# Linear attention and a gated dense layer on one core: first dense columns in six groups, with w_in in smaller pieces

## The chip, the cores and the metric

The kernel runs on one core of a Trainium2 chip. The metric is the device time of one execution in microseconds (us); lower is better. Three runs of the kernel before gave 297.32, 297.68 and 297.74 us, a median of 297.68. The profiled execution took 297.12 us, and its span, from the first to the last recorded instruction, is 295.4 us.

Engine names in what follows: PE is TensorE's matmul, PEld its weight load, DVE is VectorE, ACT is ScalarE, POOL is GpSimd, SP is SyncE. A "q" after a name is that engine's queue of DMA issues.

## The reference: what is computed

There are 8 batches, 8 heads, 576 positions and 64 channels per head. Each head computes a linear attention without softmax, then an RMS norm over its 64 channels. The heads are laid side by side as 512 features of 4608 tokens, and a two-layer dense block with a sigmoid gate follows.

```python
kv  = einsum('bhsd,bhse->bhde', k, v)          # 64 x 64 for each head
out = einsum('bhsd,bhde->bhse', q, kv)
rms = sqrt(mean(out * out, axis=-1) + 1e-6)
x   = (out / rms * g_norm)                      # -> [4608, 512]
h   = x @ w_in                                  # [512, 2048]
g   = h * (1 / (1 + exp(-1.702 * h)))
y   = g @ w_out                                 # [2048, 512] -> [4608, 512] f32
```

## The kernel before

Matmuls take float16 and accumulate in float32. Two heads make a pair, and each batch has four pairs. Of each batch's 576 positions, 512 form one dense tile; the remaining 64 of all eight batches together form a ninth tile, `x_rem`. While dense tile t runs on TensorE, the attention of batch t+1 is interleaved with it: the lists `units1` and `units2` name what is emitted after which group of hidden columns and after which step of the projection.

PSUM has eight banks, given to three pools: three for attention (`ps_a`), three for hidden columns (`ps_h`), two for outputs (`ps_o`).

```python
ps_a = ctx.enter_context(tc.tile_pool(name="ps_a", bufs=3, ...))
ps_h = ctx.enter_context(tc.tile_pool(name="ps_h", bufs=3, ...))
ps_o = ctx.enter_context(tc.tile_pool(name="ps_o", bufs=2, ...))
```

A pair's norm: the squares go through a matmul with ones, which gives the sums over each head; then two activations on ScalarE give the reciprocal root, and one VectorE instruction scales.

```python
def ss(self, c, table=False):
    ...
    nc.tensor.matmul(t[:, 0:n], ones2, sq[:, 0:n], start=True, stop=True)
    nc.scalar.activation(ln[:, 0:n], t[:, 0:n], AFT.Ln, bias=eps_t, scale=1.0 / D)
    nc.scalar.activation(rs[:, 0:n], ln[:, 0:n], AFT.Exp, bias=0.0, scale=-0.5)

def apply(self, c):      # x = out * g * rs
    nc.vector.scalar_tensor_tensor(self.x[:, c, :], o, g_col, rs, op0=ALU.mult, op1=ALU.mult)
```

The first batch's attention is emitted pair by pair. `busy(n)` issues n matmuls whose result nobody reads; they keep TensorE occupied. Then the weights and batch 1 are loaded on the GpSimd queue, which converts from float32 to float16 on the way.

```python
busy(12)
...
a0.q(0)
busy(2)
for c in range(NPAIR):
    a0.kv(c)
    busy(2)
    a0.out(c)
    if c:
        a0.ss(c - 1)
    if c > 1:
        a0.apply(c - 2)
    if c + 1 < NPAIR:
        a0.q(c + 1)
        busy(1)
busy(2)
a0.ss(NPAIR - 1)
a0.apply(NPAIR - 2)
a0.apply(NPAIR - 1)
load_w_in(0, 4)              # in blocks of 128 columns of w_in
load_w_in(4, 8)
load_w_in(8, 16)
early_load("q", 1, 0, 4)
load_w_out(0, 8)             # in blocks of 128 rows of w_out
early_load("k", 1, 0, 4)
early_load("v", 1, 0, 4)
load_w_out(8, 12)
load_w_out(12, 16)

def third():                 # batch 2, after the last of w_out has landed
    nc.gpsimd.tensor_copy(after, w_out_sb[0:1, FO - 1, 0:1])
    nc.sync.dma_start(out=after, in_=g_norm[0:1].unsqueeze(1))
    load_batch(2)
```

The dense tile. In the first two tiles the first four groups of hidden columns are open at once (`group`), with the contraction index `ko` outside, so that work can begin while later pairs of x are still being made. `deep` (tile 0 alone) runs the projection in quarters of the contraction, over all four row blocks `mo`, so that it can begin on the first rows of w_out.

```python
for i in range(group):
    hs.append(ps_h.tile(...) if i < 3 else ps_o.tile(...))
for ko in range(KO):
    for fo in range(group):
        hidden(hs[fo], fo, ko)
for fo in range(group):
    gate(hs[fo], fo)
for fo in range(FO):
    if fo >= group:
        h = ps_h.tile([P, SM], F32, name="hT", tag="hT")
        for ko in range(KO):
            hidden(h, fo, ko)
        gate(h, fo)
...
def project(mo, fo):
    ...
    nc.tensor.matmul(os[mo], gT[:, fo, mo * P : (mo + 1) * P], w_out_sb[:, fo, :], ...)
    if fo == FO - 1:
        (nc.scalar.copy if deep and mo % 2 else nc.vector.tensor_copy)(osb[:, mo, :], os[mo])
        if t == B:                       # the ninth tile stores row block by row block
            for g in range(2):
                ...
                nc.sync.dma_start(out=rows, in_=osb[g * R : (g + 1) * R, mo, :])

if deep:
    steps = [(mo, 4 * i + k) for i in range(4) for mo in range(4) for k in range(4)]
```

Batch 1 inside tile 0, with its places in the list of 64 projection steps:

```python
for c in range(NPAIR):
    at1(12, of(1, "pack_q", c))
    at2(9 + 3 * c, of(1, "q", c))
    at2(12, of(1, "pack_k", c))
    at2(23 + c, of(1, "kv", c))
    at2(30 + 8 * c, of(1, "out", c))
    at2(38 + 8 * c, of(1, "ss", c))
    at2(38 + 8 * c, of(1, "apply", c))
at2(14, third)
```

Of the kernel before, what the change touches and what calls it, by code (L numbers as in the profile page):

```python
# [8 lines left out]
F32 = mybir.dt.float32  # L9
# [3 lines left out]
P = 128  # L13
# [3 lines left out]
def kernel(  # L17
# [10 lines left out]
    nc = tc.nc  # L28
# [8 lines left out]
    SM = 512  # L37
# [67 lines left out]
    def load_batch(b):  # L105
        tiles = {}
        for n in "kvq":
            t = tiles[n] = stage.tile([P, H, J * D], F32, name=f"{n}f", tag=f"{n}f")
            nc.sync.dma_start(
                out=t, in_=srcs[n][b, :, 0:SM, :].rearrange("h (p j) d -> p h (j d)", j=J)  # L110
            )
# [76 lines left out]
    class Attention:  # L188
# [24 lines left out]
        def keep_kv(self):  # L213
            for hl in range(2):
                r = slice(hl * D, (hl + 1) * D)
                nc.vector.tensor_copy(self.kb[r, :, r], self.kvp[r, :, r])  # L216
# [41 lines left out]
        def ss(self, c, table=False):  # L258
            if table:
                nc.scalar.preload_act_table_set("natural_log_exp_and_others")  # L260
# [5 lines left out]
            nc.scalar.activation(ln[:, 0:n], t[:, 0:n], AFT.Ln, bias=eps_t, scale=1.0 / D)  # L266
            rs = attn.tile([P, SM], F32, name="rs", tag="rs", bufs=2)
# [58 lines left out]
    class Second(Attention):  # L326


        def pack_q(self, c):
            pack("q", qbuf, c)  # L330
# [4 lines left out]
        def kv(self, c):  # L335
            if c == 0:
                self.kvp = ps_a.tile([P, NPAIR, P], F32, name="kvp", tag="att")
# [10 lines left out]
            if c == NPAIR - 1:  # L348
                self.keep_kv()
# [17 lines left out]
    def dense(t, units1, units2, group, deep):  # L367
# [16 lines left out]
        for i in range(group):  # L384
            if i < 3:
                hs.append(ps_h.tile([P, SM], F32, name="hT", tag="hT"))
            else:
                hs.append(ps_o.tile([P, SM], F32, name="hO", tag="o"))
        if group:
            for ko in range(KO):  # L390
                for u in units1.get(("ko", ko), ()):
                    u()
                for fo in range(group):
                    hidden(hs[fo], fo, ko)
# [14 lines left out]
        def project(mo, fo):  # L409
# [10 lines left out]
            if fo == FO - 1:  # L420
                (nc.scalar.copy if deep and mo % 2 else nc.vector.tensor_copy)(osb[:, mo, :], os[mo])  # L421
                if t == B:
                    for g in range(2):
# [6 lines left out]
                        nc.sync.dma_start(out=rows, in_=osb[g * R : (g + 1) * R, mo, :])  # L430
# [53 lines left out]
    for c in range(NPAIR):  # L484
        a0.kv(c)
        busy(2)
        a0.out(c)
        if c:
            a0.ss(c - 1)
        if c > 1:  # L490
            a0.apply(c - 2)
        if c + 1 < NPAIR:
            a0.q(c + 1)
            busy(1)
    busy(2)
    a0.ss(NPAIR - 1)
    a0.apply(NPAIR - 2)
    a0.apply(NPAIR - 1)
    load_w_in(0, 4)
    load_w_in(4, 8)  # L500
    load_w_in(8, 16)
    early_load("q", 1, 0, 4)
    load_w_out(0, 8)
    early_load("k", 1, 0, 4)
    early_load("v", 1, 0, 4)
    load_w_out(8, 12)
    load_w_out(12, 16)


    after = const.tile([1, 1], F32)  # L510

    def third():
        nc.gpsimd.tensor_copy(after, w_out_sb[0:1, FO - 1, 0:1])
        nc.sync.dma_start(out=after, in_=g_norm[0:1].unsqueeze(1))
        load_batch(2)
# [6 lines left out]
    for t in range(NT):  # L522
# [12 lines left out]
        if t == 0:  # L535
            at1(4, of(0, "out", NPAIR))
# [6 lines left out]
            for c in range(NPAIR):  # L543
                at1(12, of(1, "pack_q", c))
                at2(9 + 3 * c, of(1, "q", c))
                at2(12, of(1, "pack_k", c))
                at2(23 + c, of(1, "kv", c))
                at2(30 + 8 * c, of(1, "out", c))
                at2(38 + 8 * c, of(1, "ss", c))
                at2(38 + 8 * c, of(1, "apply", c))  # L550
            at2(14, third)
        elif b < B:
            if t == 1:
                at2(46, of(1, "out", NPAIR))
# [16 lines left out]
        dense(t, u1, u2, 4 if t < 2 else 0, t == 0)  # L571
# [30 lines left out]
```

## Time and profile before

| | |
|---|---|
| median of three runs | 297.68 us |
| span of the profiled execution | 295.4 us |
| TensorE busy | 286.7 us, 97% of the span |
| ScalarE busy | 175.1 us, 59% |
| VectorE busy | 90.4 us, 31% |
| granted TensorE clock | 0.998 of full |
| HBM read and written | 36.70 MB and 9.44 MB |

The profile's page cuts the span into 40 equal slices of some 7.4 us. Each digit is a busy share in tenths (9 is 90% or more); the last row is what the DMA engines moved, in GB/s.

```profile
PE   7989999999999999999999999999999999999993
ACT  2696428868765875587467756775667565026300
GB/s 181 203 209 206 204 117 365 254 199 363 371 245 197 355 13 196 265 244 1 159 227 315 4 126 98 0 3 53 169 0 2 0 142 2 0 89 54 2 71 71
```

The first slice and the last are where TensorE is not full. For some five slices the transfers run evenly at about 205 GB/s: these are the loads on the GpSimd queue, counted by the bytes written. In the rows of waits quoted further on, the numbers after a name are the waiting time in total, the number of waits and the longest. In timeline rows they are the start and the duration in us, and what ended an idle time stands in brackets. In rows of DMA issues the last number is the median time from issue to landing.

### The profile page before, as it was taken

The page shows a single profiled execution, that of the slowest core. Times are in us where ns is not written, and L with a number is a line of the kernel's source. Part 1 is how long each engine was busy: PE and PEld are TensorE (multiplying, and loading weights), DVE is VectorE, ACT ScalarE, POOL GpSimd, SP SyncE. Part 2 cuts the span into 40 slices and gives each one's busy share as a digit, 9 for nine tenths or more (in the row PEclk, how much of TensorE's full clock was granted, in tenths as well). Part 3 has the DMA queues.
Part 4 walks back from the last instruction along what each step waited for, and adds up shares of the span by engine and source line. Part 5 has one row for each costly group of instructions (what it writes and reads, how often), then busy time and mean ns, then how long its engine had stood idle before and what let it go on. Part 6 is the DMA issues. An engine that isn't in the chain of part 4 may idle for free.

```text
span 295.4 us, 3904 instructions
## 1 busy us (share of the span) xinstructions
PE 286.7 (97%) x1551; PEld 134.2 (45%) x1551; DVE 90.4 (31%) x194; ACT 175.1 (59%) x283; POOL 23.6 (8%) x42
## 2 busy tenths in 40 slices
PE   7989999999999999999999999999999999999993
PEld 3434454454445444544454445444454444444441
DVE  3531415613461246114602461145314300110020
ACT  2696428868765875587467756775667565026300
POOL 8540000200220020001000200000000000000000
PEclk9999999999999999999999999999999999999999
DMA  8999969889988906870489034001600030021033
GB/s 181 203 209 206 204 117 365 254 199 363 371 245 197 355 13 196 265 244 1 159 227 315 4 126 98 0 3 53 169 0 2 0 142 2 0 89 54 2 71 71
DMA packets 53863, 42.65 MB, mean 144 GB/s; under 512 B 24916, under 2 KB 51028, under 8 KB 53076
## 3 DMA queue, kind: packets, MB, share of 16 engines
q1 hardware_dynamic: 45730, 34.81, 39.4%
q0 software_dynamic: 7904, 7.29, 15.1%
q10 hardware_dynamic: 210, 0.30, 0.3%
q8 instruction: 12, 0.20, 0.3%
q14 instruction: 7, 0.06, 0.1%
HBM read 36.70 MB, written 9.44 MB: 156 GB/s over the span
## 4 chain that ended last, share of the span: by engine, by line
PE 87%; DMA 7%; ACT 3%; DVE 1%; issue 0%; POOL 0%
PE o L413 41%; PE hT L372 36%; DMA w_out_sb<-in_moe_w_out_dram 6%; PE ss L264 3%; PE outT L235 2%; PE kvp L201 2%; DMA qf<-in_q_dram 2%; PE idle L468 1%; ACT ln L266 0%; PE kvp L341 0%; PE kvp L209 0%; ACT L381 0%; ACT rs L268 0%; PE q L314 0%; ACT sq L255 0%
## 5 line engine op out<-in xcount | busy, mean ns | idle before, releaser
L413 PE MATMUL o<-w_out_sb,gT 128*128 128x512 f16 x576 | 137.4, 379 | 0.5 <-DMA w_out_sb<-in_moe_w_out_dram 0.5
L381 ACT ACTIVATE gT<-hT 128x512 f16<-128x512 f32 x142 | 84.5, 598 | 69.2 <-PE hT L372 69.1
L372 PE MATMUL hT<-xT,w_in_sb 128*128 128x512 f16 x504 | 115.4, 379 | 1.2 <-DMA w_in_sb<-in_moe_w_in_dram 1.0
L413 PEld LDWEIGHTS <-gT 128*128 128x128 f16 x576 | 55.5, 98 | 65.4 <-issue 2.0
L372 PEld LDWEIGHTS <-w_in_sb 128*128 128x128 f16 x576 | 55.2, 98 | 64.0 <-DMA w_in_sb<-in_moe_w_in_dram 1.7
L274 DVE SCALAR_TENSOR_TENSOR xT<-outT,g_col,rs 128x512 f16<-128x512 f32 x32 | 24.0, 750 | 63.6 <-ACT rs L268 63.6
L421 DVE COPY osb<-o 128x512 f32<-128x512 f32 x34 | 23.3, 684 | 60.8 <-PE o L413 60.8
L266 ACT ACTIVATE ln<-ss,eps_t 128x512 f32<-128x512 f32 (+1 forms) x40 | 25.8, 644 | 15.9 <-PE ss L264 15.8
L255 ACT ACTIVATE sq<-outT 128x512 f16<-128x512 f32 (+1 forms) x40 | 21.7, 543 | 11.5 <-PE outT L235 11.2
L268 ACT ACTIVATE rs<-ln 128x512 f32<-128x512 f32 (+1 forms) x40 | 23.5, 587 | 1.3
L216 DVE CAST kvb<-kvp 64x256 f16<-64x256 f32 x14 | 5.9, 422 | 45.7 <-PE kvp L209 43.0
L264 PE MATMUL ss<-sq,ones 128*128 128x512 f16 (+1 forms) x40 | 14.3, 357 | 0.0
L372 PE MATMUL hT<-x_rem,w_in_sb 128*128 128x512 f16 x64 | 14.0, 379 | 0.0
L136 POOL CAST krem<-krf 64x512 f16<-64x512 f32 x6 | 4.1, 678 | 111.1 <-DMA krf<-in_k_dram 85.6
L381 ACT ACT_TABLE_LOAD x8 | 10.3, 1283 | 0.1
L131 DVE CAST qbuf<-qf 128x512 f16<-128x512 f32 x24 | 9.4, 453 | 2.5 <-DMA qf<-in_q_dram 2.5
L468 PE MATMUL idle<-kvb 128*128 128x512 f16 x27 | 8.9, 442 | 1.3 <-DVE kvb L149 1.3
L201 PEld LDWEIGHTS <-kbuf 128*128 128x128 f16 x96 | 7.4, 98 | 5.7
L201 PE MATMUL kvp<-vbuf,kbuf 128*128 128x128 f16 x96 | 9.3, 219 | 0.0
L235 PE MATMUL outT<-qTd,kvb 128*128 128x512 f16 x24 | 9.1, 379 | 0.0
L260 ACT ACT_TABLE_LOAD x7 | 9.0, 1283 | 0.1
L131 DVE CAST kbuf<-kf 128x512 f16<-128x512 f32 x24 | 8.7, 425 | 0.0
(56 smaller groups left out, 88.0 us busy)
## 6 DMA issues: line engine op xcount, KB each, us to landing
kf<-in_k_dram SPq DMA_DIRECT2D x6, 1024.0 KB, 5.6
vf<-in_v_dram SPq DMA_DIRECT2D x6, 1024.0 KB, 8.1
qf<-in_q_dram SPq DMA_DIRECT2D x6, 1024.0 KB, 10.3
out_dram<-osb SPq DMA_DIRECT2D x6, 1024.0 KB, 4.2
out_dram<-osb SPq DMA_DIRECT2D x12, 128.0 KB, 2.4
out_dram<-osb SPq DMA_DIRECT2D x6, 192.0 KB, 3.0
w_in_sb<-in_moe_w_in_dram POOLq DMA_DIRECT2D x2, 512.0 KB, 8.9
w_in_sb<-in_moe_w_in_dram POOLq DMA_DIRECT2D x1, 1024.0 KB, 13.7
```

What stands on the lines that cost most here:

```text
L131: nc.vector.tensor_copy(out=dst[:, c, :, :].rearrange("p j (l d) -> p j l d", l=2), in_=src[n][:, h, :].rearrange("p l (j d) -> p j l d", ...
L201: nc.tensor.matmul(t[:, c, :].rearrange("p (l d) -> p l d", l=2), kh[:, c, j, :], vh[:, 2 * c : 2 * c + 2, j * D : (j + 1) * D], start=(j ...
L235: nc.tensor.matmul(t.rearrange("p c r -> p (c r)"), self.kb[:, c, :], self.qT[c][:, 0:SM], start=True, stop=True,)
L255: nc.scalar.activation(sq[:, 0:n], t, AFT.Square)
L264: nc.tensor.matmul(t[:, 0:n], ones2, sq[:, 0:n], start=True, stop=True)
L266: nc.scalar.activation(ln[:, 0:n], t[:, 0:n], AFT.Ln, bias=eps_t, scale=1.0 / D)
L268: nc.scalar.activation(rs[:, 0:n], ln[:, 0:n], AFT.Exp, bias=0.0, scale=-0.5)
L274: nc.vector.scalar_tensor_tensor(self.x[:, c, :], o, g_col, rs, op0=ALU.mult, op1=ALU.mult)
L372: nc.tensor.matmul(h, w_in_sb[:, ko, fo * P : (fo + 1) * P], x[:, ko, :], start=(ko == 0), stop=(ko == KO - 1),)
L381: nc.scalar.activation(gT[:, fo, :], h, AFT.Gelu_apprx_sigmoid)
L413: nc.tensor.matmul(os[mo], gT[:, fo, mo * P : (mo + 1) * P], w_out_sb[:, fo, :], start=(fo == 0), stop=(fo == FO - 1),)
L421: (nc.scalar.copy if deep and mo % 2 else nc.vector.tensor_copy)(osb[:, mo, :], os[mo])
```

## The change

The change rearranges the first 50 us and the end.

- The first dense tile opens six groups of hidden columns instead of four. The groups come in an order that follows the arrival of w_in: first groups 0 and 1, then 2 and 3, over the first two pairs of x, then 4 and 5, and last the fourth pair of x for all six. Accordingly w_in comes first in three pieces of two blocks each (512 KB of float32) and then in pieces of four and six blocks. The two further banks come from the output and attention pools.
- The sums of a pair (`sums`: matmul and Ln) are split from its scaling (`rs`: Exp), so that in the first batch's attention the activations of neighbouring pairs can be interleaved. The order of the pairs' steps is written out, with three fewer `busy` matmuls.
- Batch 1 comes by halves: k and v of two pairs at a time, their kv products kept two pairs at a time, at new places in the list of steps, and their sums in the banks of the hidden columns. w_out comes by quarters between them.
- Batch 2's load waits for the second half of batch 1's v instead of the last of w_out.
- In the ninth tile each output block is copied half by VectorE and half by ScalarE, and its two stores go out on the SyncE and the ScalarE queue.

```diff
-    def load_batch(b):
+    def load_batch(b, landed=None):
...
+            if landed is not None and n == "k":
+
+                nc.gpsimd.tensor_copy(t[0:1, 0, 0:1], landed)
...
-        def keep_kv(self):
+        def keep_kv(self, c0=0, c1=NPAIR):
...
-                nc.vector.tensor_copy(self.kb[r, :, r], self.kvp[r, :, r])
+                nc.vector.tensor_copy(self.kb[r, c0:c1, r], self.kvp[r, c0:c1, r])
...
         def ss(self, c, table=False):
+            self.sums(c, table)
+            self.rs(c)
+
+        def sums(self, c, table=False):
...
     class Second(Attention):
+        ss_pool = (ps_h, "hT")
...
-            if c == 0:
+            if c % 2 == 0:
                 self.kvp = ps_a.tile([P, NPAIR, P], F32, name="kvp", tag="att")
...
-            if c == NPAIR - 1:
-                self.keep_kv()
+            if c % 2:
+                self.keep_kv(c - 1, c + 1)
...
-            if i < 3:
-                hs.append(ps_h.tile([P, SM], F32, name="hT", tag="hT"))
+            pool, tag = (ps_h, "hT") if i < 3 else (ps_o, "o") if i < 5 else (ps_a, "att")
+            hs.append(pool.tile([P, SM], F32, name="hG", tag=tag))
+        if group:
+            if t == 0:
+                order = [(ko, fo) for f in (0, 2) for ko in (0, 1) for fo in (f, f + 1)]
+                order += [(2, fo) for fo in range(4)]
+                order += [(ko, fo) for ko in (0, 1, 2) for fo in (4, 5)]
+                order += [(KO - 1, fo) for fo in range(group)]
             else:
-                hs.append(ps_o.tile([P, SM], F32, name="hO", tag="o"))
...
+                order = [(ko, fo) for ko in range(KO) for fo in range(group)]
+            for ko, fo in order:
+                hidden(hs[fo], fo, ko)
...
-                (nc.scalar.copy if deep and mo % 2 else nc.vector.tensor_copy)(osb[:, mo, :], os[mo])
+                if t == B:
+                    half = DM // 2
+                    nc.vector.tensor_copy(osb[:, mo, 0:half], os[mo][:, 0:half])
+                    nc.scalar.copy(osb[:, mo, half:DM], os[mo][:, half:DM])
...
-                        nc.sync.dma_start(out=rows, in_=osb[g * R : (g + 1) * R, mo, :])
+                        queue = (nc.sync, nc.scalar)[g]
+                        queue.dma_start(out=rows, in_=osb[g * R : (g + 1) * R, mo, :])
...
-    for c in range(NPAIR):
-        a0.kv(c)
...
+    a0.kv(0)
     busy(2)
+    a0.out(0)
+    a0.q(1)
+    a0.ss(0)
+    a0.kv(1)
+    a0.q(2)
+    a0.out(1)
+    busy(1)
+    a0.kv(2)
+    busy(2)
+    a0.out(2)
+    a0.apply(0)
+    a0.ss(1)
+    a0.q(3)
+    a0.sums(2)
+    busy(1)
+    a0.kv(3)
+    a0.apply(1)
+    busy(2)
+    a0.out(3)
+    a0.rs(2)
+    busy(2)
+    a0.ss(3)
+    a0.apply(2)
+    a0.apply(3)
+    for f in (0, 2, 4):
+        load_w_in(f, f + 2)
+    load_w_in(6, 10)
+    load_w_in(10, FO)
+    load_w_out(0, 4)
+    early_load("q", 1, 0, NPAIR)
+    load_w_out(4, 8)
+    for c in (0, 2):
+        early_load("k", 1, c, c + 2)
+        early_load("v", 1, c, c + 2)
+        load_w_out(8 + 2 * c, 12 + 2 * c)
...
-            at1(4, of(0, "out", NPAIR))
+            at1(7, of(0, "out", NPAIR))
...
-                at2(12, of(1, "pack_k", c))
-                at2(23 + c, of(1, "kv", c))
-                at2(30 + 8 * c, of(1, "out", c))
-                at2(38 + 8 * c, of(1, "ss", c))
-                at2(38 + 8 * c, of(1, "apply", c))
-            at2(14, third)
+                at2((21, 21, 36, 36)[c], of(1, "pack_k", c))
+                at2((23, 24, 43, 44)[c], of(1, "kv", c))
+                o = (27, 33, 47, 52)[c]
+                at2(o, of(1, "out", c))
+                at2(o + 7, of(1, "ss", c))
+                at2(o + 7, of(1, "apply", c))
+            at2(14, load_batch, 2, vbuf[0:1, NPAIR - 1, 0:1])
...
-        dense(t, u1, u2, 4 if t < 2 else 0, t == 0)
+        dense(t, u1, u2, (6, 4)[t] if t < 2 else 0, t == 0)
```

## The prediction

> **What bounds the kernel now.** I read the page's shares first, then TensorE's waits, then the stretches in which those waits lie, in order of time.
>
> ```profile
> PE 286.7 (97%) x1551; PEld 134.2 (45%) x1551; DVE 90.4 (31%) x194; ACT 175.1 (59%) x283; POOL 23.6 (8%) x42
> PE 87%; DMA 7%; ACT 3%; DVE 1%; issue 0%; POOL 0%
> ```
>
> TensorE is busy for 97% of the span and carries 87% of the chain that ended last. The matmul work is the same in both kernels, so a gain can only come from TensorE's gaps, from work that is not the kernel's own (fillers), and from what stands before its first and after its last needed matmul. The list of TensorE's waits for the whole span is short:
>
> ```profile
> PE hT L372 <- DMA w_in_sb<-in_moe_w_in_dram: 1.0, 1, 1.0
> PE o L413 <- DMA w_out_sb<-in_moe_w_out_dram: 0.5, 1, 0.5
> PE hT L372 <- ACT gT L381: 0.2, 1, 0.2
> ```
>
> In the timeline these waits stand here:
>
> ```profile
> 14.10 0.59 PE L468 MATMUL idle<-kvb 128*128 128x512 f16 x2
> 14.73 0.38 PE L264 MATMUL ss<-sq,ones 128*128 128x512 f16 x1
> 16.09 0.82 PE L372 MATMUL hT<-xT,w_in_sb 128*128 128x512 f16 x3 [0.98 <-DMA w_in_sb<-in_moe_w_in_dram]
> ...
> 30.86 1.25 PE L413 MATMUL o<-w_out_sb,gT 128*128 128x512 f16 x5 [0.47 <-DMA w_out_sb<-in_moe_w_out_dram]
> ```
>
> The dense layer starts at 16.09 because the first piece of w_in lands then. From that point to the last matmul's end at 290.4 I compared each matmul's start with the one before it, at 0.216 us for 512 columns (64 steady matmuls take 13.81 us in the chain). What exceeds that pace is only 2.8 us in 274: 0.63 at 30.86, about 0.2 at 19.75, about 1.0 in all between 40 and 54 (the largest 0.25 at 40.31 behind the copies of kvb and 0.31 at 53.36 behind a gate), and 0.11 in each of six later tiles. So the early weight loads and the tail are the whole prize.
>
> The loads:
>
> ```profile
> w_in_sb<-in_moe_w_in_dram POOLq DMA_DIRECT2D x2, 512.0 KB, 8.9
> w_in_sb<-in_moe_w_in_dram POOLq DMA_DIRECT2D x1, 1024.0 KB, 13.7
> w_out_sb<-in_moe_w_out_dram POOLq DMA_DIRECT2D x1, 1024.0 KB, 16.8
> q0 software_dynamic: 7904, 7.29, 15.1%
> q8 instruction: 12, 0.20, 0.3%
> ```
>
> Sizes count the f16 written (7.29 MB; a "512 KB piece" of f32 is 256 KB here). The casting queue runs in order at a steady 205 GB/s from 5.5 to 41.8 us (windows: 205, 207, 205 and 205 GB/s from 20 to 40). In the trace its landings are: batch 0's last tile 12.49, w_in 16.04, 17.90 and 22.86, q of batch 1 25.75, half of w_out 30.81, k 33.70, v 37.01, the rest of w_out 39.25 and 41.78. 512 KB at 205 GB/s is 2.56 us, so the first piece was due at 15.05. Fifteen of its sixteen semaphore steps came by 15.08 and the last at 16.04: the packet records show a 16 KB packet of the instruction queue from 13.95 to 14.84. I take it that this packet held one DMA engine for 0.9 us.
>
> The tail:
>
> ```profile
> 290.40 0.69 DVE L421 COPY osb<-o 128x512 f32<-128x512 f32 x1 [2.76 <-PE o L413]
> 280.76 11.46 SPq L430 DMA_DIRECT2D out_dram<-osb  x8
> ```
>
> After the last matmul: a copy of 0.69 us, two issues in a row on the same queue (0.47 and 0.60, starting 291.12 and 291.63), the second store landing at 293.99, and 1.36 us of ending.
>
> **What the Trainium skill says.** "Runtime: NRT & Kernel Launch", section Instruction fetch mechanics: an engine's instructions come by DMA in blocks of 16 KiB, 256 instructions. The trace agrees: 12 packets of 16,384 bytes on queue 8 for TensorE's some 3,100 instructions. "DMA: Bandwidth & Descriptors", section Issuing engines are not separate DMA queues: all queues share the 16 DMA engines, and a second issuing engine saves only issue time. I therefore credit the second store queue with its 0.5 us and no bandwidth. The same page, Specifications, gives 512 bytes as the least transfer for full rate. The new pieces write runs of 256 f16, exactly 512 bytes; before, runs were 768 to 2048 bytes, so no run here shows it. "TensorE: Matmul & The Clock Gate", Part 1, says the clock halves after an idle window of about 3.4 us. The granted clock here is 1.00 across the 0.98 us wait, and I expect no gap longer than that, so dropping three fillers should not cool it.
>
> **The change part by part.**
>
> *Start.* I laid out the new order by hand with the old kernel's distances: square to the next activation 0.5, Ln to its own Exp 0.72, Ln to another function 0.55, sum matmul to Ln 0.42, kv to its VectorE product 0.42, product to out 0.35, out to square 0.43. Up to the first square (8.29) nothing changes. Then sums of pair 0 at 8.93, out of pair 1 at 9.92, kv of pair 2 at 10.36 (v lands 10.31), out 11.13, sums of pair 1 at 11.35; ScalarE: square 2 at 11.56, Ln 1 12.06, Exp 1 12.78, Ln 2 13.33. kv of pair 3 waits for Ln 1's bank, 12.8; out 13.57, square 3 14.0, Exp 2 14.5; the last sums 14.65, Ln 3 15.07, Exp 3 15.79. So the first dense matmul can go at 14.87 instead of 16.09: **1.2 us**. x of pairs 0 and 1 is ready by then, x of pair 2 at 15.92, of pair 3 at 17.2. The new order asks for pair 2 after 8 matmuls (16.6) and pair 3 after 18 (18.76): both are in time.
>
> The loads must keep up. A first piece of 256 KB needs 1.3 us after 12.49, say 1.4 for its shorter runs: 13.9, before 14.87. The second is due at 15.3 and wanted at 15.73; the instruction packet probably falls on it or on the third, since TensorE has run about as many instructions by then, and would make it 16.1. I charge **0.15** for that. The third is due 16.7, wanted 17.46. Pieces 6 to 10: due 19.4, wanted 20.06. Pieces 10 to 16: due 23.2, wanted 23.5. The margins are thin.
>
> *Gate.* With six groups open there are 6 x 4 x 0.216 = 5.2 us of matmul before a bank must come free, instead of 3.45. The table load ends near 17.7 and the first gate near 19.7, before the next tile at 20.06: the **0.2 us** at 19.75 goes.
>
> *w_out.* 64 matmuls and the four rest products end at 14.87 + 13.8 + 0.1 = 28.8 (29.0 with the charge). The first quarter of w_out, now ahead of q, lands at 23.2 + 2.5 = 25.7. The **0.63 us** at 30.86 goes. Later deadlines, adding 2.5 us per quarter and 1.45 per half of k or v: q 28.6 (wanted 30.9), second quarter 31.2 (33.2), first k and v 34.1 (35.1), third quarter 36.6 (37.9), second k and v 39.5 (40.7), last quarter 42.0 (42.6).
>
> *Batch 1 by halves.* The same matmuls, one more pair of smaller copies to kvb, beside other work. The first out stands 0.65 us of matmuls behind the kv, and the two half copies need about 0.8: some 0.15 twice instead of 0.25 once. Sums come at step 59 instead of 62, so the gelu table comes earlier and the 0.31 at 53.36 about halves. I credit **0.3** over this stretch.
>
> *Batch 2's load* is released by v of batch 1 (39.5) instead of by w_out (41.78, issue 42.38). Its transfers took 2 us to reach full rate, so it meets only the last of w_out: nothing gained, some risk.
>
> *Tail.* Two half copies side by side take about 0.42 instead of 0.69, and the second issue no longer follows the first, 0.51: **0.8 us**.
>
> Sum: 1.2 - 0.15 + 0.2 + 0.63 + 0.3 + 0.8 = 3.0 us. 297.7 - 3.0 = **294.7 us**.
>
> **The rivals.** First, the DMA stream takes over as the bound. Everything TensorE wants in the first 42 us is already 7.29 MB at 205 GB/s, and my margins are 0.3 to 1 us. If 512-byte runs went at 150 GB/s, the three pieces would take 1.4 us more, every deadline from the fourth piece on would slip past its need once, and about 1 us of the gain would be lost: 295.7. For it: the rate per run size is unknown. Against: rates at 768 to 2048 bytes are within a few per cent. Second, the wait moves to ScalarE or to PSUM banks: six groups, the split sums and the second batch's sums in the hT banks tie TensorE to single activations (the sums of pair 1 of batch 1 wait for pair 0's Ln with no time to spare). Several stalls of 0.2 to 0.4 would make 295.5 to 296. Third, batch 2's early load slows the last quarter of w_out: both share the DMA engines, and a quarter at half rate would land up to 2 us late, 296. Against it is the slow ramp. Fourth, better than I think: if the instruction packet falls between pieces and ScalarE keeps the denser order, 293.8.
>
> **Range and chances.** All rivals cost 1 to 1.5 us singly, and misses are likelier late than early: 293.7 to 296.2. Faster by 2% needs 291.7, twice the sum of all gaps I found: 0.01. Slower by 2% needs a stall of 9 us against my estimate: 0.01. Within 2%: 0.98.
>
> **What would show it.** The first hG matmul near 14.9, the first o near 28.9 without a w_out wait, the last matmul's end near 288, the last store issued 0.05 us after its half copies on both queues. I am wrong if the first dense matmuls wait on w_in again, if a w_in or w_out wait appears in the third or a later piece, or if new ACT waits on TensorE add up to over 1 us.

## The result, and the profile after

The changed kernel takes **295.82 us** (median of four runs, 295.23 to 296.51) against 297.71 us for the kernel before on the same chip (297.32 to 297.81): a ratio of 0.994, 95% interval 0.9913 to 0.9967. A second set of five runs gave 295.96 us. The prediction was 294.7 us, a gain of 3.0 us; the gain is 1.9 us. It is inside the predicted range, but by a different sum than the one I wrote down.

The page of the changed kernel, its shares (part 1), the engines' shares of the chain that ended last (part 4), one queue (part 3) and the weight loads (part 6: size of each, median us to landing):

```profile
PE 286.4 (98%) x1548; PEld 134.1 (46%) x1548; DVE 89.6 (31%) x196; ACT 176.2 (60%) x287; POOL 26.9 (9%) x47
...
q0 software_dynamic: 9008, 7.29, 15.8%
...
PE 96%; ACT 2%; DVE 1%; issue 0%
...
w_out_sb<-in_moe_w_out_dram POOLq DMA_DIRECT2D x4, 512.0 KB, 16.9
...
w_in_sb<-in_moe_w_in_dram POOLq DMA_DIRECT2D x3, 256.0 KB, 6.8
```

DMA stood for 7% of the chain and has left it; TensorE went from 87% to 96%. The same 7.29 MB are now 9008 packets instead of 7904, at nearly the same cost (15.8% against 15.1%). TensorE's waits of the changed kernel (us in total, number, longest), where before a load of w_in (1.0), one of w_out (0.5) and a gate (0.2) stood:

```profile
PE idle L490 <- DVE kvb L152: 1.3, 1, 1.3
PE ss L271 <- ACT sq L258: 0.6, 2, 0.3
PE kvp L354 <- DVE kbuf L93: 0.4, 1, 0.4
```

All three of those are gone. The first two rows here lie before the dense layer. One new wait is on the list: the kv product of batch 1 for a packed k. The start of the dense layer, and the place of that wait, in TensorE's timeline (start, us, then the work; what ended an idle time stands in brackets):

```profile
14.95 0.38 PE L271 MATMUL ss<-sq,ones 128*128 128x512 f16 x1 [0.25 <-ACT sq L258]
15.17 5.34 PE L385 MATMUL hG<-xT,w_in_sb 128*128 128x512 f16 x24
...
42.04 0.51 PE L354 MATMUL kvp<-vbuf,kbuf 96*128 96x128 f16 x6 [0.39 <-DVE kbuf L93]
```

The 24 matmuls of the six groups run without a break, from 15.17 instead of 16.09. The tail, in the timeline of all engines:

```profile
288.99 0.42 DVE L438 COPY osb<-o 128x256 f32<-128x256 f32 x1 [3.03 <-PE o L428]
289.45 0.37 ACT L439 COPY osb<-o 128x256 f32<-128x256 f32 x1 [3.08 <-DVE osb L438]
289.85 0.47 SPq L452 DMA_DIRECT2D out_dram<-osb  x1
289.85 0.50 ACTq L452 DMA_DIRECT2D out_dram<-osb  x1
```

ScalarE's half copy begins after VectorE's half copy has ended, and what released it was that copy. The two stores are issued together, but 0.90 us after the last matmul's end (288.95); before, the single copy let the first go after 0.76.

The two profiled executions differ by 1.89 us of span (295.35 and 293.46). By the traces it is made up so; a plus is time saved:

| step | predicted | in the profile |
|---|---|---|
| first dense matmul, 16.09 to 15.17 | 1.2 | 0.92 |
| an instruction packet on an early piece of w_in | -0.15 | 0 |
| wait for the first gate, 0.20 at 19.75 | 0.2 | 0.20 |
| wait for w_out, 0.63 at 30.86 | 0.63 | 0.63 |
| stalls between 30 and 54 us, 0.99 to 1.33 | 0.3 | -0.34 |
| last matmul's end to the last landing, 3.63 to 3.52 | 0.8 | 0.11 |
| last landing to the end of the span, 1.36 to 0.99 | none named | 0.37 |
| sum | 3.0 | 1.89 |

This execution took 295.23 us and was the fastest of its four. Part of what the slower ones pay in addition is the subject of the first and of the fifth experiment.

### The profile page after: what moved, and what is told of

Same layout as the page of the kernel before. It is cut to its first block, busy times and chain, and to the rows that moved or that the text cites. A ratio compares the mean times of both kernels' runs of the same rounds, so it can differ in the third digit from the quotient of the medians.

```text
span 293.5 us, 3915 instructions
## 1 busy us (share of the span) xinstructions
PE 286.4 (98%) x1548; PEld 134.1 (46%) x1548; DVE 89.6 (31%) x196; ACT 176.2 (60%) x287; POOL 26.9 (9%) x47
## 3 DMA queue, kind: packets, MB, share of 16 engines
q1 hardware_dynamic: 45408, 34.28, 42.9%
q0 software_dynamic: 9008, 7.29, 15.8%
## 4 chain that ended last, share of the span: by engine, by line
PE 96%; ACT 2%; DVE 1%; issue 0%
PE o L428 42%; PE hT L385 39%; PE hG L385 3%; PE ss L271 3%; PE outT L238 2%; PE idle L490 2%; PE kvp L204 2%; ACT sq L258 1%; ACT ln L273 1%; PE kvp L354 1%; PE kvp L212 0%; ACT rs L279 0%; PE q L367 0%; PE kv L308 0%; PE outT L249 0%; DVE xT L285 0%
## 5 line engine op out<-in xcount | busy, mean ns | idle before, releaser
L394 ACT ACTIVATE gT<-hT 128x512 f16<-128x512 f32 x134 | 80.0, 599 | 67.5 <-PE hT L385 67.5
L385 PE MATMUL hT<-xT,w_in_sb 128*128 128x512 f16 x472 | 107.2, 379 | 0.0
L442 DVE COPY osb<-o 128x512 f32<-128x512 f32 x30 | 20.5, 684 | 37.2 <-PE o L428 37.2
L219 DVE CAST kvb<-kvp 64x256 f16<-64x256 f32 (+1 forms) x16 | 6.2, 389 | 43.1 <-PE kvp L212 42.0
L271 PE MATMUL ss<-sq,ones 128*128 128x512 f16 (+1 forms) x40 | 14.3, 357 | 0.7 <-ACT sq L258 0.6
L438 DVE COPY osb<-o 128x256 f32<-128x256 f32 x4 | 1.7, 425 | 25.7 <-PE o L428 25.7
L385 PE MATMUL hG<-xT,w_in_sb 128*128 128x512 f16 x40 | 9.1, 379 | 0.0
```

The lines of the kernel that those rows point to most:

```text
L385: nc.tensor.matmul(h, w_in_sb[:, ko, fo * P : (fo + 1) * P], x[:, ko, :], start=(ko == 0), stop=(ko == KO - 1),)
L394: nc.scalar.activation(gT[:, fo, :], h, AFT.Gelu_apprx_sigmoid)
L442: copy(osb[:, mo, :], os[mo])
```

## The experiments

Theory after this profile: the lost microsecond lies in the tail (copies of one bank one after the other), in batch 1 (a copy queued on VectorE behind another that waits) and in the instruction packet, which sometimes hits the second piece of w_in. The rivals were that the loads as such are too slow, and that ScalarE's new order holds TensorE. All twelve kernels are compared with the kernel before (297.7 us); where nothing else is said they start from the changed kernel.

### 1. The changed kernel again

No edit.

> The changed kernel once more, for the spread of its times and a second trace. Its first four times went from 295.23 to 296.51, against 297.32 to 297.81 before. Theory: the small margins of the loads make some executions wait where others do not; a second trace then shows the same distances between events everywhere except at one or two waits for w_in, w_out or batch 1. Rival: the spread comes from the start, before the first matmul, and all later distances are the same. Expected median 295.8, 295.2 to 296.5.

Measured: 295.96 us (295.73 to 296.35), ratio 0.9946 [0.9934, 0.9959]. TensorE's timeline at the start of this profile:

```profile
15.30 1.02 PE L385 MATMUL hG<-xT,w_in_sb 128*128 128x512 f16 x4
16.94 4.49 PE L385 MATMUL hG<-xT,w_in_sb 128*128 128x512 f16 x20 [0.62 <-DMA w_in_sb<-in_moe_w_in_dram]
```

Here the dense layer stops after four matmuls: 0.78 us beyond the steady pace, for the second piece of w_in, which landed at 16.89 instead of 15.41. In both executions a 16 KB packet of the instruction queue starts near 14.7 and takes 0.9 us on one DMA engine. In the first it delayed the third piece (landed 17.24, harmless), here the second. So one and the same program has two outcomes, I take it by which piece is in flight on that engine at that moment. Such a packet appears in every trace of the study, and the piece it meets lands 1.1 to 1.6 us after the packet's end: in the kernel before the packet starts at 13.95 and the first piece lands at 16.04, in the first profile of the changed kernel 14.71 and 17.24, here 14.70 and 16.89.

The rival, a spread from the start, fails for this pair of traces (first out at 8.00 and 8.08), but it holds for others. In the 14 traces of the study the granted clock became full between 4.0 and 7.3 us. Where that was by 5.7 us, the first out began at 7.51 to 8.08. Where it was at 6.5 us or later (experiments 3, 6, 7, 8, 9 and 11), all twelve of the first fillers ran at 0.43 us each, and the first out began at 8.39 to 8.70.

### 2. Whole copies in the ninth tile, both queues kept

```diff
-                if t == B:
-                    half = DM // 2
-                    nc.vector.tensor_copy(osb[:, mo, 0:half], os[mo][:, 0:half])
-                    nc.scalar.copy(osb[:, mo, half:DM], os[mo][:, half:DM])
-                else:
-                    copy = nc.scalar.copy if deep and mo % 2 else nc.vector.tensor_copy
-                    copy(osb[:, mo, :], os[mo])
+                copy = nc.scalar.copy if deep and mo % 2 else nc.vector.tensor_copy
+                copy(osb[:, mo, :], os[mo])
```

> The changed kernel with the ninth tile's blocks copied whole by VectorE as before, stores still on two queues. Theory (the half copies run one after the other, 0.42 + 0.37 with a handover, because the second waits for the first): from the last matmul's end to the last store's landing 3.4 us instead of 3.5, so 0.1 us faster than the changed kernel. Rival (half copies overlap in part, and the two queues do not help): 0.2 to 0.3 us slower than the changed kernel.

Measured: 295.91 us (295.57 to 296.16), ratio 0.9941 [0.9927, 0.9954], the same as the changed kernel. From the last matmul's end to the last landing it takes 3.39 us, with the halves 3.52. The half copies gain nothing; by the trace they cost 0.13.

### 3. The old tail: whole copies, all stores on SyncE

```diff
-                        queue = (nc.sync, nc.scalar)[g]
+                        queue = nc.sync
```
and whole copies as in experiment 2.

> The changed kernel with the whole tail of before: whole copies on VectorE, all stores on the SyncE queue. Theory: last matmul's end to last landing 3.63 us as before, 0.1 us more than in the changed kernel, and the ending after it 0.3 us longer because SyncE then waits for all stores: about 0.4 us slower in the span. Rival (my prediction's 0.8 for the tail was right and the loss lies elsewhere): 0.8 us slower.

Measured: 296.30 us (296.01 to 296.64), ratio 0.9958 [0.9943, 0.9974]; last matmul's end to last landing 3.66 us, against 3.39 with two queues. So the second queue is worth 0.27 in the trace, about half of the 0.5 that I had given it. The store itself takes longer when two queues store at once, 2.63 us from issue to landing instead of 2.39, which takes back half of the 0.51 us that its issue comes earlier. One thing fell with this run: the end after the last landing stays short (0.93 us), though all stores are on one queue again. The trace shows what is in it. SyncE closes the program with a row of checks of semaphores, one every 0.06 us. In the kernel before, eight of them stand behind the landing of the last store, in the changed kernel two, here one, and the end takes 1.36, 0.99 and 0.93 us. So the 0.37 us are six checks: which place in the row the last store's semaphore happens to have.

### 4. The last block in two PSUM banks

```diff
+            halves = t == B and mo == 3
+            if fo == 0 and halves:
+                os[mo] = [
+                    ps_o.tile([P, DM // 2], F32, name="oa", tag="o"),
+                    ps_h.tile([P, DM // 2], F32, name="ob", tag="hT"),
+                ]
...
+            for i in range(2 if halves else 1):
+                n = slice(i * DM // 2, (i + 1) * DM // 2) if halves else slice(0, DM)
```
Each matmul of that block becomes two of 256 columns, and each engine copies its own bank.

> The changed kernel with the last output block split into two PSUM banks of 256 columns (two matmuls of 256 columns instead of one of 512 in its 16 steps), so that the second half copy waits for its own matmul alone. Theory: both half copies start within 0.15 us of each other, the last store is issued about 0.45 us after the last matmul's end instead of 0.90, and the landing comes 0.35 to 0.45 us earlier; the 32 shorter matmuls cost about 0.1. Rival (VectorE and ScalarE cannot read PSUM side by side at full rate): each half copy takes 0.6 or more and nothing is won.

Measured: 295.71 us (295.23 to 297.01), ratio 0.9942 [0.992, 0.9964]. The profiled execution was the slowest, 297.01. Its timeline, in the tail and at its longest stop:

```profile
97.08 0.38 PE L238 MATMUL outT<-qTd,kvb 128*128 128x512 f16 x1 [1.33 <-DMA qTd<-qbuf]
...
291.12 0.42 DVE L446 COPY osb<-oa 128x256 f32<-128x256 f32 x1 [2.96 <-PE oa L436]
291.23 0.37 ACT L447 COPY osb<-ob 128x256 f32<-128x256 f32 x1 [2.66 <-DMA out_dram<-osb]
```

In two banks the half copies start 0.11 us apart, each as long as alone (0.42 and 0.37), and the last landing comes 3.06 us after the last matmul's end instead of 3.52. So sharing the bank was what put them in a row; as each bank is here also a tile of its own, the run does not separate the bank from the tile. The median shows little of this gain of 0.46 (295.71 against 295.96 in experiment 1) and the profiled execution none, because something else cost it more: 1.49 us beyond the pace at 97.08, for the transposed q of batch 3. It was 0 in the first profile of the changed kernel, 0.20 in experiment 1 and 0.44 in experiment 2.

### 5. The staging tiles at their old addresses

Why should q of batch 3 be late? It lands 11.3 us after its issue before (73.61 to 84.87), 12.8 in the changed kernel (74.36 to 87.15), 13.9 in experiment 4. The bytes are the same. The change drops the four-byte tile `after` from the constant pool; with it all staging tiles, and the tiles behind them, move down by 32 bytes per partition. The staging tiles stood at multiples of 1024 (kf at 92160), and now do not (92128). The edit puts an unused tile back:

```diff
+    pad = const.tile([1, 1], F32)
+    nc.vector.memset(pad, 0.0)
```

> The changed kernel with one unused 4-byte tile put back where the removed tile 'after' stood, so that all staging tiles lie 32 bytes higher, as in the kernel before (kf at 92160, a multiple of 1024, instead of 92128). Theory: the shift by 32 bytes made the float32 loads of later batches slower (packets of 1024 bytes took 46 to 56 ns instead of 46, of 256 bytes 18 to 45 instead of 18), which made batch 3's transposed q late. Then packets fall back to 46 and 18 ns, batch 3's q lands within 11.5 us of its issue instead of 12.8 to 13.9, the wait of the fourth tile's first out for its transposed q (0 to 1.5 us in five traces) is gone, and the median falls by 0.2 to 0.5 us, to about 295.5, with a smaller spread. Rival (the slower packets come from the earlier start of batch 2's load beside the weights, not from the address): packets stay at 46 to 56 and nothing changes.

Measured: 295.48 us (295.31 to 295.61), ratio 0.9927 [0.9914, 0.9939]. Rows of the page for the changed kernel (queue 1: packets, MB, share of the engines' time; q loads: median us to landing):

```profile
q1 hardware_dynamic: 45408, 34.28, 42.9%
...
qf<-in_q_dram SPq DMA_DIRECT2D x6, 1024.0 KB, 12.5
```

and for this run:

```profile
q1 hardware_dynamic: 45408, 34.28, 38.9%
...
qf<-in_q_dram SPq DMA_DIRECT2D x6, 1024.0 KB, 11.1
```

The same packets and bytes take 38.9% instead of 42.9%. In the packet records the 1024-byte packets after 60 us take 48.3 ns on the mean instead of 52.5 (90th percentile 46 ns and 56 ns). The stall at the transposed q is gone, the median is 0.4 us better, and the runs lie within 0.3 us instead of 1.3 (0.6 in experiment 1). None of the five traces of the changed order at the old addresses (experiments 5 and 9 to 12) has that stall, and of the six at the moved ones three have it.

The first batch pays too, since its first pair comes through the staging tiles. Packets of 1536 bytes before 6 us took 85 to 90 ns on the mean in the seven traces at the old addresses and 92 to 98 in the seven at moved ones, and the last tile of batch 0 landed at 12.21 to 12.55 us and at 12.64 to 12.91. Here the first out begins at 7.86 and the dense layer at 15.02, against 8.00 and 15.17 in the changed kernel.

### 6. The kernel before, with its staging tiles shifted

The same two lines put into the kernel before, which move its staging tiles up by 32 bytes (kf at 92192).

> The kernel before with one more unused 4-byte tile, which moves the staging tiles 32 bytes up, off the multiple of 64 (kf at 92192). Theory (address): its packets of 1024 bytes take 46 to 56 ns and of 256 bytes up to 45, as in the changed kernel, and batch 3's q needs 12.5 to 13.5 us; the time rises by 0 to 0.8 us, 297.7 to 298.5. Rival (order of loads): packets stay at 46 and 18 ns, time 297.7.

Measured over 20 runs: 297.97 us (297.64 to 298.25), ratio 1.001 [1.0003, 1.0017].

```profile
q1 hardware_dynamic: 45730, 34.81, 43.2%
```

In the kernel before this queue's row shows 39.4%. So the shift, and nothing else of the change, makes the packets slower, in either direction. Here it costs only 0.3 us. The trace has no stall at batch 3's q, and from the first projection to the last matmul's end it takes as long as the kernel before (259.49 and 259.50 us), so the loss lies ahead of that; how much of it is the address this trace cannot tell, because its clock also became full late.

### 7. Fewer instructions ahead of the dense layer

Meant to move the instruction packet: the kernel before without the 13 filler matmuls of the first batch's attention.

```diff
         a0.kv(c)
-        busy(2)
         a0.out(c)
...
             a0.q(c + 1)
-            busy(1)
-    busy(2)
```

> The kernel before without the 13 filler matmuls after the first two groups (26 instructions of TensorE fewer before the dense layer). Theory: TensorE's instruction packet comes at its 271st recorded instruction, so it now comes some 13 dense matmuls later, after the first piece of w_in has landed; that piece lands at 15.1 instead of 16.04 and the dense layer starts about 0.9 us earlier, at 15.2; 296.8 us. Rival (the piece was late for another reason, or fillers keep the clock up): first dense matmul at 16.0, or matmuls at half speed, 297.7 or more.

Measured: 298.33 us (297.8 to 299.47, 13 runs), ratio 1.0031 [1.002, 1.0043]. For its purpose it is a miss: the packet still came at 13.99 and the first piece of w_in at 16.17. Only 249 instructions of TensorE had started before it, against 271 in the kernel before, so it does not come at a fixed count of TensorE's instructions. What sets its time stays open. The run showed something else. A stretch of the timeline, and the busy time, granted clock (third from the end) and DMA by stage:

```profile
16.22 0.95 PE L372 MATMUL hT<-xT,w_in_sb 128*128 128x512 f16 x3 [1.19 <-DMA w_in_sb<-in_moe_w_in_dram]
```

```profile
16.20:20.30 4.10, 4.08 (x12) 1.54 (x13) 2.26 (x6) 2.12 (x3) 1.71 (x3) 0.58 1.15 212
20.30:24.40 4.10, 4.06 (x23) 1.86 (x22) 0.00 (x0) 3.32 (x7) 0.00 (x0) 1.00 1.23 205
```

For four microseconds the granted clock is 0.58 on the mean (half from 16.8 to 20.2 us), and from 16.96 to 20 a matmul comes every 0.43 us instead of every 0.216. Twelve matmuls ran in a time in which the kernel before ran 19. In the 3.4 us before the clock fell, TensorE had been busy for 1.56 us (2.38 in the same stretch of the kernel before, whose clock stayed full), and its longest idle time was the 1.19 in the row.

### 8. The packing of k three steps earlier

```diff
-                at2((21, 21, 36, 36)[c], of(1, "pack_k", c))
+                at2((21, 21, 33, 33)[c], of(1, "pack_k", c))
```

In the changed kernel VectorE's own timeline shows why the third kv of batch 1 waits:

```profile
40.97 0.75 DVE L285 SCALAR_TENSOR_TENSOR xT<-outT,g_col,rs 128x512 f16<-128x512 f32 x1 [3.86 <-ACT rs L279]
41.64 0.62 DVE L93 COPY kbuf<-kraw 96x768 f16<-96x768 f16 x2
```

The raw k had landed at 38.32. The copies that pack it stand behind the scaling of pair 0 in VectorE's queue, and that has its Exp only at 40.94; VectorE was idle for 3.86 us until then.

> The changed kernel with the packing of batch 1's second half of k emitted at step 33 instead of 36, ahead of the first scaling of batch 1 in VectorE's queue. Theory: the stall of 0.55 us at the third kv of batch 1 (at 42 to 43 us in all five traces) comes from packing that stands behind a scaling which waits for its Exp; it vanishes, and 295.3 is the median. Rival (the load of k is late): the stall stays, since the packing cannot start before 38.4.

Measured: 296.15 us (295.78 to 299.45, seven runs), ratio 0.9974 [0.9943, 1.0004]: unclear by the times, which two runs of 297.35 and 299.45 widen. The trace decides:

```profile
44.35 0.39 PE L238 MATMUL outT<-qT,kvb 128*128 128x512 f16 x1 [0.54 <-DVE kvb L219]
```

The 0.55 at 42 is gone, and the next out waits 0.70 instead of 0.20 for the copies of kvb, which now stand behind the scaling of pair 1. The stall moved by 2.3 us and the stretch from the first projection to the last is unchanged (259.42 against 259.48).

### 9. The first batch's attention in the order of the kernel before

From here on each kernel starts from that of experiment 5.

```diff
+    for c in range(NPAIR):
+        a0.kv(c)
+        busy(2)
+        a0.out(c)
+        if c:
+            a0.ss(c - 1)
+        if c > 1:
+            a0.apply(c - 2)
+        if c + 1 < NPAIR:
+            a0.q(c + 1)
+            busy(1)
```
in place of the written-out order; sums and scaling of a pair stand together again.

> The changed kernel with the 32 bytes put back (as e5) and with the first batch's attention in the order of before, sums and scaling together and three more fillers. Theory (only the smaller first pieces of w_in let the dense layer start earlier; TensorE was ready at 15.1 in the old order too): first dense matmul 7.2 to 7.3 us after the first out, as in e5 (7.16); x of pair 2 comes 0.5 us later than in e5, so up to 0.3 us of waits among the first 24 dense matmuls; within 0.3 us of e5, 295.5 to 295.8. Rival (the interleaved activations bring the start forward, as my prediction counted): start 0.9 us later than e5, 296.3.

Measured: 295.63 us (295.46 to 295.70), ratio 0.9931 [0.9914, 0.9948], against 295.48 [0.9914, 0.9939] in experiment 5.

```profile
15.57 5.42 PE L387 MATMUL hG<-xT,w_in_sb 128*128 128x512 f16 x24
```

The whole start is later here (first out at 8.49, in experiment 5 at 7.86); from first out to the first dense matmul it takes 7.08 us, with the new order 7.16. The interleaving of the activations brings nothing that can be measured.

### 10. w_in in the pieces of the kernel before

```diff
-    for f in (0, 2, 4):
-        load_w_in(f, f + 2)
-    load_w_in(6, 10)
-    load_w_in(10, FO)
+    load_w_in(0, 4)
+    load_w_in(4, 8)
+    load_w_in(8, 16)
```

> The changed kernel with the 32 bytes put back (as e5) and with w_in in the pieces of before, 512, 512 and 1024 KB, everything else as changed. Theory: the first piece is due 2.6 us after the last tile of batch 0 (15.1), and the instruction packet at 14.1 to 14.7 falls on it, so it lands at 16.2 to 16.6, 1.2 to 1.35 us after the packet's end; the first dense matmul comes 1.1 to 1.4 us later than in e5, but then no wait for the second piece (0.42 to 0.78): 0.5 to 0.9 us slower than e5, 296.0 to 296.4. Rival (piece size does not matter, the packet does not hold the piece): first piece at 15.1 and the start as in e5.

Measured: 296.39 us (296.24 to 296.53), ratio 0.9958 [0.9944, 0.9973]: 0.9 us slower than experiment 5.

```profile
16.02 5.35 PE L387 MATMUL hG<-xT,w_in_sb 128*128 128x512 f16 x24 [1.19 <-DMA w_in_sb<-in_moe_w_in_dram]
```

The first piece landed at 15.97; its packet of instructions began at 13.73. The last piece is waited for as well, 0.21 us at 23.45. The gain at the start comes from the small first piece. It has landed (13.8 to 14.3 in all runs with small pieces) before the packet's hold can reach it.

### 11. A version put together from the findings

The kernel of experiment 5 with the two banks of experiment 4, the early packing of experiment 8, the scaling of pair 1 behind the copies of kvb, and an order of the six groups that runs three pairs of x on the first two groups before it needs the second piece:

```diff
-                order = [(ko, fo) for f in (0, 2) for ko in (0, 1) for fo in (f, f + 1)]
-                order += [(2, fo) for fo in range(4)]
-                order += [(ko, fo) for ko in (0, 1, 2) for fo in (4, 5)]
+                order = [(ko, fo) for f in (0, 2, 4) for ko in (0, 1, 2) for fo in (f, f + 1)]
...
-                at2(o + 7, of(1, "apply", c))
+                at2((o + 7, 45, o + 7, o + 7)[c], of(1, "apply", c))
```

> e5 with four more edits: pair 2 of the first two groups ahead of groups 2 and 3 in the first dense tile (gives the second piece of w_in 0.43 us more); k of batch 1's second half packed at step 33 and the second scaling of batch 1 moved to step 45, behind the copies of kvb; the last output block in two PSUM banks. Expected against e5: the wait for the second piece 0.4 us shorter where it is waited for, but 0.2 us for pair 2; the 0.55 us at the third kv gone without the 0.5 us that e8 paid two steps later; 0.3 us less at the end. Sum 0.9 us: 294.6, between 294.2 and 295.1. Rival (the stall only moves again, VectorE's queue being full there): 295.1 or more.

Measured: **294.30 us** (294.19 to 295.04, four runs), ratio 0.9894 [0.9877, 0.991]. It is faster than both kernels. The four edits were not run one by one; what each gives is read from the trace. The profiled execution was the slowest of the four, and its start was late (first out at 8.59, in experiment 5 at 7.86). In it the last landing follows the last matmul's end by 3.04 us (3.52 in the changed kernel); first to last projection takes 259.06 us (259.48), with 0.20 left at 44.04 and no stall at 42; and the second piece, hit by the packet, landed at 16.57, where the new order pays 0.23 for it instead of 0.3 to 0.8.

### 12. Four groups instead of six

```diff
-                order += [(ko, fo) for ko in (0, 1, 2) for fo in (4, 5)]
...
-        dense(t, u1, u2, (6, 4)[t] if t < 2 else 0, t == 0)
+        dense(t, u1, u2, (4, 4)[t] if t < 2 else 0, t == 0)
```

> The changed kernel with the unused four-byte tile of e5, but with four groups instead of six in the first batch's dense layer; the small pieces of w_in and all else stay. Theory (six groups only remove the wait for the first gate): after 16 matmuls the fifth column tile needs a bank that the first gate frees about 0.2 us later, so a wait of 0.2 us stands near 18.7 to 19.1 and the time is 0.2 us above e5's 295.48: about 295.7. Rival (six groups are what lets the loads keep up): with four groups the third piece of w_in and those behind it are wanted earlier, waits on w_in of 0.5 us or more appear, 296 or above. Second rival (the groups bring nothing): the bank is free in time, no wait, 295.5.

Measured: 295.72 us (295.33 to 295.99), ratio 0.9934 [0.9921, 0.9948]; experiment 5 has 295.48. The intervals overlap. The trace has the wait of the theory, 0.20 us beyond the pace at the fifth column tile:

```profile
18.90 3.40 PE L387 MATMUL hT<-xT,w_in_sb 128*128 128x512 f16 x15
```

No later piece of w_in is waited for. So six groups remove the gate's 0.2 us and do nothing for the loads.

## Why the prediction was right, and where it was not

**What bounds it** held. All the gain lies in TensorE's gaps at the start, in the tail and in the ending, and the matmul work did not change.

**Start, 1.2: mis-sized, and partly for the wrong reason.** The term is right in kind: 0.92 in the profile. Of the 0.30 between 14.87 and 15.17, 0.13 is the whole start lying later (first out at 8.00 instead of 7.87). That goes with the moved staging tiles: experiment 5, with the old addresses, has 7.86 and a gain of 1.07 here. The other 0.17 are small slips in the chain that I had laid out by hand. But I derived the 14.87 from the interleaved activations, and experiments 9 and 10 show that the pieces alone carry it: old order with small pieces 295.63, new order with large pieces 296.39. My own rows said so. In the kernel before, TensorE had finished its last sums at 15.11 (14.73 and 0.38) and idled 0.98 us for w_in; the order of the activations was never what ended last there.

**The packet, 0.15: mis-sized.** I charged it once as a small shift of the second piece. When it falls on that piece, the stall is 0.2 to 0.8 us (0.78, 0.70, 0.65, 0.42 and 0.30 in experiments 1, 2, 4, 5 and 12, and 0.23 in the order of experiment 11); in experiments 8 and 9 TensorE started late enough to miss it, and on the third piece it is nothing (first profile, experiment 3). So the prediction's own sign of being wrong, first dense matmuls that wait on w_in again, is absent from the first profile and present in these six. That is a part of the spread of this kernel. The reason I gave for the packet's place, that TensorE has run about as many instructions by then, fell with experiment 7. "Runtime: NRT & Kernel Launch" of the Trainium skill, section Instruction fetch mechanics, calls the cost of crossing a block mostly hidden. For TensorE's own instructions the first profile agrees: it ran 24 matmuls in 5.34 us, without a break, across the end of the packet at 15.60. For the load that meets the packet the traces do not. The second piece lands 1.29 us after the first where the packet misses it, and 2.1 to 2.7 us after it where the packet falls on it. That the packet is the cause rests on its place in all traces. Experiment 7 was to move it and did not, so it is argued and not forced.

**Gate, 0.2, and w_out, 0.63: as predicted.** Both are gone in every trace with six groups; experiment 12 brings back the first alone. The first projection starts at 29.09, for 28.9.

**Later deadlines: as predicted.** Pieces of w_in landed at 14.12, 15.41, 17.24, 19.66 and 23.40 (13.9, 15.3, 16.7 plus the packet, 19.4, 23.2), the quarters of w_out at 25.96, 31.61, 37.07 and 42.31 (25.7, 31.2, 36.6, 42.0), v at 34.32 and 39.78 (34.1, 39.5). The first rival is thereby false: runs of 512 bytes go as fast as longer ones, since the second piece of 256 KB came 1.29 us after the first, which is 203 GB/s. The third is false too, since the last quarter came within 0.3 us of its time with batch 2's load under way.

**Batch 1 by halves, +0.3: wrong in sign, -0.34.** The copies to kvb cost 0.20 twice, near the 0.15 that I counted, and the 0.31 at 53.36 shrank to 0.20. The step that failed is "beside other work", with the deadline "second k and v 39.5 (40.7)": I had compared each need with the landings of the loads only. The second half of k had landed at 38.32 and still held TensorE for 0.55 us at 42.04, because in VectorE's queue its packing stood behind the scaling of pair 0, which got its Exp at 40.94. Experiment 8 moved the wait to the copies of kvb, and experiment 11, which also moved the scaling of pair 1, removed it. The second rival named this kind of loss, but looked for it on ScalarE and in the banks.

**Tail, 0.8: wrong, 0.1 up to the landing.** The step that failed is "two half copies side by side take about 0.42 instead of 0.69". They take 0.42 and then 0.37, because both read one bank. The Trainium skill states it, and I had not looked it up: "PSUM — Partial Sum Buffer", section PSUM bank collisions raise a hardware error, says that two engines must not access a bank at the same time in the same quarter of its rows, and that the compiler makes the one wait for the other, ScalarE and VectorE included. The trace agrees (0.46 between their starts in one bank, 0.11 in two). So the last store is issued 0.90 us after the last matmul's end and not at about 0.5. The second queue was credited with 0.5 and is worth 0.27: two stores issued together took up to 2.63 us to land, the last of two in a row 2.36 to 2.39. In exchange there came 0.37 after the last landing that no step had named: six checks of semaphores fewer (experiment 3). That was luck.

**Not in the prediction: the address of the staging tiles.** I read the removal of `after` as the removal of a wait. It moved the targets of some 18 MB of later loads (six of 1 MB each for k, v and q) by 32 bytes, where packets are slower. That costs some 0.4 us in the median (experiment 5) and goes with part of the spread: the times of one kernel lie 0.24 to 0.85 us apart in the five experiments with the changed order at the old addresses, and 0.6 to 3.7 at the moved ones. Experiments 5 and 6 show the slower packets in both kernels.

**Fillers.** "Dropping three fillers should not cool it" held: the granted clock is 1.00 from 15 to 20 us. Dropping 13 of them in the kernel before does cool it (experiment 7). The 3.4 us of idle time that I had quoted would not have foretold that, since no idle time was over 1.2 us.

The total stayed in the range because the two early waits were sure and large, because every miss was below 0.8 us, and because 0.37 us came by luck. Without the last the gain of the profiled execution is 1.5 us, half of the 3.0.

## What to carry to other kernels

Before you call a new instruction "beside other work", find its place in its engine's queue and ask what the instruction ahead of it waits for; a landed load is not enough. Two engines emptying one PSUM bank took turns here, so a block that is to be split between them must be computed in two banks. When a change drops or adds a small tile, compare the addresses of the large ones behind it, and keep tiles that receive many DMA packets where they were.

## What the runs showed of the hardware that I had not expected

- Loads into SBUF tiles moved by 32 bytes from a multiple of 1024, down or up, took 7 to 9% longer per 1024-byte packet (48.3 to 48.6 ns on the mean at the old addresses, 52.1 to 52.5 moved) and 17 to 24% longer per 256-byte packet (20.7 to 20.9 and 24.6 to 25.7 ns), in the traces of both kernels and of experiments 5 and 6. Shifts other than 32 bytes were not run. The queue's share of the DMA engines went from 39.4% to 43.2% in the kernel before, and from 42.9% back to 38.9% in the changed one.
- Where a 16 KB instruction packet of 0.9 to 1.0 us falls on the second piece of w_in, that piece lands 0.8 to 1.5 us later after the first than where it does not (2.1 to 2.7 us instead of 1.29).
- With TensorE busy for 1.56 of 3.4 us and no idle time over 1.2 us, the granted clock fell to half for the next 3.4 us. With 2.38 of 3.4 us busy it stayed full.
- The granted clock became full 4.0 to 7.3 us after the start of the span, under the same twelve filler matmuls, and the first out of a late one began at 8.39 us or later.
- VectorE and ScalarE copying 256 columns each from two banks at once were no slower than one after the other: 0.42 and 0.37 us.
- SyncE's checks of semaphores at the end of the program took 0.06 us each, and how many of them stood behind the last store's landing (eight, two or one) went with an ending of 1.36, 0.98 to 0.99 or 0.93 us in all 14 traces.
